# First batch's recurrence in half chunks of 64 tokens, in an mLSTM cell with Fourier mixing and an MLP

## The chip, the cores and the metric

One NeuronCore of a Trainium2 chip runs the whole program. The metric is the device time of one execution in microseconds (us); lower is better. Five engines take part, each with its own queue that is worked off in order: PE multiplies matrices into PSUM, DVE and ACT work on vectors (ACT also evaluates functions such as exp and tanh), POOL is a slower vector engine[...], and SP only issues DMAs. An instruction that waits for another engine holds everything behind it in its own queue.

## The reference

All inputs are float32. Batch B = 4, heads H = 8, tokens S = 768, head width D = 40, model width 320.

```python
def _attn_ref(q, k, v, i_gate, f_gate, o_gate):
    ...
    for t in range(S):
        kt, vt, qt = (k[:, :, t], v[:, :, t], q[:, :, t])
        m_new = np.maximum(f_gate[:, :, t] + m, i_gate[:, :, t])
        f_stab = np.exp(f_gate[:, :, t] + m - m_new)
        i_stab = np.exp(i_gate[:, :, t] - m_new)
        m = m_new
        C = f_stab[:, :, None, None] * C + i_stab[:, :, None, None] * np.einsum('bhd,bhe->bhde', vt, kt)
        n = f_stab[:, :, None] * n + i_stab[:, :, None] * kt
        h_tilde = np.einsum('bhde,bhe->bhd', C, qt)
        nq = np.einsum('bhd,bhd->bh', n, qt)[:, :, None]
        denom = np.maximum(np.abs(nq), 1.0)
        o = 1.0 / (1.0 + np.exp(-o_gate[:, :, t]))
        y[:, :, t] = o * h_tilde / denom

def _moe_ref(x, w_ch1, w_ch2):
    X = np.fft.fft(x, axis=1)
    X = np.fft.fft(X, axis=2)
    mixed = np.real(X).astype(np.float32)
    u = x + mixed
    mu = np.mean(u, axis=-1, keepdims=True)
    var = np.mean((u - mu) ** 2, axis=-1, keepdims=True)
    un = (u - mu) / np.sqrt(var + 1e-06)
    ch = np.maximum(un @ w_ch1, 0.0) @ w_ch2
    return (u + ch).astype(np.float32)
```

The output y of the cell, with its heads side by side, is the input x of the mixing stage.

## The kernel before

**Stages of a batch.** The recurrence over tokens is worked in six chunks of 128 tokens. Within a chunk, queries meet keys in a score matrix that is weighed with exponentials of gates and masked to the past; what came before the chunk arrives through a state of 40 x 41 numbers a head (the 41st column carries n). Then come the Fourier mixing (products with cosine and sine tables), the normalisation, and the two MLP products. The recurrence of batch b + 1 runs beside the MLP of batch b. Batch 0 has nothing to run beside: its gates, recurrence and mixing stand alone at the front.

**Two forms of the recurrence.** Batches 1 to 3 use `halves_*`: a chunk is two halves of 64 tokens; scores, state updates, from-state and from-chunk products are 64x64 tiles of PE, four of which can be under way at once (`TILES`, `product`, L518). Heads of one `hip` (0 to 3, 4 to 7) share a half of the partitions. Outputs have tokens on partitions, so `mlstm_finish` (L701, DVE: denominator, output gate, product) reads them from PSUM as they are. Chunks 0, 1 and 3 (`BACKWARDS`) are held in reverse order of tokens, which the mixing wants: `mlstm_finish` leaves them in `so` and `halves_rows` (L722) moves the rows into `x` by DMA. Batch 0 uses `mlstm_*` (L522 to L611): whole chunks of 128, two heads side by side, outputs with features on partitions; ACT copies them to `hT` (`mlstm_gather`, L577), PE turns them (`mlstm_turn`, L607), and only then DVE finishes them, straight into `x`.

**Gates** (`gates`, L142). For all 32 batch-heads at once, DVE sums the forget gates (`sums`), forms the running maxima M (`maxima`). PE spreads M over partitions for batch 0 (`spread_max`, L209: a mask product, then one product a head, from chunk 2 on in three bf16 parts that POOL makes in `parts`); ACT takes the exponential a head at a time, with a per-partition bias (`mlstm_exp`, L486, 8 x 128 columns a chunk). `weights` and `decay` on ACT make the factors of keys and queries; `columns` on PE turns the former, which lands in `colT`. The factors of queries and the maxima of later batches go out to DRAM (`G_d`, `M_d`) and come back spread over partitions (`Gb`, L472; `W`, L461). `halves_of_chunks` (L322) derives the factors for halves, which the later batches need.

**The order of work** is written by hand: `at(slot, phase, fn, ...)` puts a call into a plan; slots and phases are sorted, and each engine's queue gets its instructions in that order. Phases of a slot run from `EVAC` 0 over `FILL` 1, `MAIN` 2 to `FILL_PE` 3 and beyond. `gates` issues its first part at once, before slot 0. Batch 0's recurrence has slots 0 to 21, three a chunk (`plan_mlstm`, L742); its mixing starts at 22 (`plan_mix`, with folds of chunk pairs (2,3), (1,4), (0,5) at slots 16, 19, 22: `mix_fold`, L807, fold(2), fold(1), fold(0) below), its MLP at slot 31.

**SP's queue** issues all loads, in the order of the plan: a chunk's q and k (`mlstm_load`), `so` (output gate), `Gb`, the weight pieces, and the Fourier tables (`load_tables`, L437, slot 12, 1.8 MB). The MLP weights come as 64-bit words, in pieces of 640 KB: `load` (raw), `take` (two DVE instructions), `convert` (two on ACT), `join` (three on DVE). Five pieces are for w1 (numbers 0 to 4, number 2 being the tail `w1t_sb`); lists `when` (L1348) and `early` (L1358) say when.

Of the kernel before, what the change touches and what calls it, by code (L numbers as in the profile page):

```python
# [19 lines left out]
L = 128  # L20
# [33 lines left out]
def kernel(  # L54
# [28 lines left out]
    ps_early = ExitStack()  # L83
    ps_s, ps_h = (ps_early.enter_context(tc.tile_pool(name=n, bufs=2, space=PSUM)) for n in ("ps_s", "ps_h"))

    turn = iter("3210321032120312031230123012012301023130201320132013203120123021320321")
# [17 lines left out]
    h_first = const.tile([L, NP, 1], FP, name="h_first")  # L104
# [6 lines left out]
    C_bufs = [const.tile([L, NP, L], FP, name=f"C{n}") for n in range(3)]  # L111
    states = [t.rearrange("p n t -> p (n t)")[:, i * 2 * L:(i + 1) * 2 * L] for t in C_bufs for i in range(2)]
# [3 lines left out]
    Cd_bufs = [s_last[:, n * NP * D1:(n + 1) * NP * D1].rearrange("p (n m) -> p n m", m=D1) for n in range(2)]  # L116
    hT_bufs = [const.tile([L, NP, L], FP, name=f"h{n}") for n in range(2)]
# [18 lines left out]
    def idle_products(n, first=False):  # L136
        pw = bank("pi", [L, 2 * L]) if first else ps_s.tile([L, 2 * L], FP, name="pi", tag="ps")
        for i in range(n):
            nc.tensor.matmul(pw, rest[:, 0:L], rest, start=True, stop=True, skip_group_check=True)


    def gates(gp):  # L142
        f_sb = gp.tile([BH, NT, L], FP, name="f_sb")
        free = w2_sb.rearrange("p f m -> p (f m)")
        M, a = (free[0:n, (i + 1) * S:(i + 2) * S].rearrange("p (c t) -> p c t", t=L) for i, n in enumerate((L, BH)))
        nc.sync.dma_start(out=f_sb.rearrange("p c t -> p (c t)"), in_=f_gate.rearrange("b h s -> (b h) s"))
        nc.sync.dma_start(out=a.rearrange("p c t -> p (c t)"), in_=i_gate.rearrange("b h s -> (b h) s"))
        keep = gp.tile([BH, NT, L], FP, name="keep")
        shift = gp.tile([BH, NT, L], FP, name="shift")
        m_in = gp.tile([BH, NT, 1], FP, name="m_in")  # L150
        F = gp.tile([BH, NT, L], FP, name="F")
        g, wk = (x_bufs[1].rearrange("p c m -> p (c m)")[0:n, i * S:(i + 1) * S].rearrange("p (c t) -> p c t", t=L)
                 for i, n in enumerate((L, BH)))
        nM = gp.tile([BH, NT], FP, name="nM")
        M3 = gp.tile([3 * BH, NT, L], BF, name="M3")
        below = gp.tile([BH, NT, L], BF, name="below")
        sel = gp.tile([3 * BH, BH], BF, name="sel")
        ident_b, later_b = (gp.tile([L, L], BF, name=n) for n in ("ident_b", "later_b"))
# [7 lines left out]
        nc.gpsimd.memset(later_b, 0.0)  # L166
        nc.gpsimd.affine_select(out=later_b, in_=later_b, compare_op=OP.is_ge, fill=-M_INIT, base=0, pattern=[[1, L]],
                                channel_multiplier=-1)
        nc.scalar.copy(out=ident_b, in_=ident)
        for i in range(3):  # L170
            nc.scalar.copy(out=sel[i * BH:(i + 1) * BH], in_=ident[0:BH, 0:BH])
# [3 lines left out]
        nc.vector.memset(M[:, 0:2], 0.0)  # L175
        for t in C_bufs:
            nc.scalar.copy(out=t.rearrange("p (two n) t -> p two (n t)", two=2),
                           in_=rest.unsqueeze(1).to_broadcast([L, 2, 2 * L]))
# [7 lines left out]
        w1_pieces[1].load()  # L186
        for t in hT_bufs + Cd_bufs + [h_first]:
            nc.gpsimd.memset(t, 0.0)

        def flat(t, s):  # L190
            return t[0:BH, s].rearrange("p c t -> p (c t)")
# [5 lines left out]
        def maxima(s, initial):  # L197
            c0, c1 = s.start, s.stop
            nc.vector.tensor_tensor(out=a[:, s], in0=a[:, s], in1=F[:, s], op=OP.subtract)
            if c0 > 0:  # L200
                nc.vector.tensor_copy(out=shift[:, s, 0:1], in_=F[:, c0 - 1:c1 - 1, L - 1:L])
            nc.vector.tensor_tensor_scan(out=flat(M, s), data0=flat(shift, s), data1=flat(a, s), initial=initial,
                                         op0=OP.add, op1=OP.max)
            nc.vector.tensor_scalar(out=nM[:, s], in0=M[0:BH, s, L - 1], scalar1=-1.0, scalar2=None, op0=OP.mult)
            if c0 > 0:
                nc.vector.tensor_tensor(out=m_in[:, s], in0=M[0:BH, c0 - 1:c1 - 1, L - 1:L],
                                        in1=F[:, c0 - 1:c1 - 1, L - 1:L], op=OP.add)

        def spread_max(b, c, h0):  # L209

            k = chunks[b, c]
            if h0 == 0:
                k.W = wp.tile([L, H, L], FP, name="W", tag="W")
                k.M = []
            k.M.append(bank("pM", [L, NP, L]))
            nc.tensor.matmul(k.M[-1], ident_b, later_b.unsqueeze(1).to_broadcast([L, NP, L]), start=True, stop=False,
                             skip_group_check=True)
            for h in range(h0, h0 + NP):
                bh = b * H + h
                w, x = (ident[:, bh:bh + 1], M[:, c, :]) if c < 2 else (sel[:, bh:bh + 1], M3[:, c, :])  # L220
                nc.tensor.matmul(k.M[-1][:, h - h0, :], w.to_broadcast([w.shape[0], L]), x, start=False, stop=True,  # L221
                                 skip_group_check=True)

        def parts(s):

            m, rest_ = M[0:BH, s], shift[:, s]
            nc.gpsimd.tensor_copy(out=M3[0:BH, s], in_=m)
            nc.gpsimd.tensor_tensor(out=rest_, in0=m, in1=M3[0:BH, s], op=OP.subtract)
            nc.gpsimd.tensor_copy(out=below[:, s], in_=rest_)
            nc.gpsimd.tensor_copy(out=M3[BH:2 * BH, s], in_=rest_)  # L230
            nc.gpsimd.tensor_tensor(out=M3[2 * BH:, s], in0=rest_, in1=below[:, s], op=OP.subtract)

        def spread_decay(b, c):
            k = chunks[b, c]
            k.G = bank("pG", [L, NP, L])
            for h in range(H):
                r, bh = slice(h % 2 * 64, (h % 2 + 1) * 64), b * H + h
                nc.tensor.matmul(k.G[r, h // 2, :], ident[:, bh:bh + 1].to_broadcast([L, 64]), g[:, c, :],
                                 start=True, stop=True)

        def weights(s):
            for c in range(s.start, s.stop):
                nc.scalar.activation(out=wk[:, c], in_=a[:, c], func=AF.Exp, bias=nM[:, c:c + 1])

        def decay(s):
            for c in range(s.start, s.stop):
                nc.scalar.activation(out=g[0:BH, c], in_=M[0:BH, c], func=AF.Exp, scale=-1.0, bias=m_in[:, c])

        def columns(s, j):
            pt = ps_h.tile([L, NT, BH], FP, name="pt", tag="ph")  # L250
            for c in range(s.start, s.stop):
                nc.tensor.transpose(pt[:, c, :], (a, wk)[j][:, c, :], ident[0:BH, 0:BH])
            return pt

        first, others, last = slice(0, 1), slice(1, NT), slice(2, NT)
        sums(first)
        maxima(first, M_INIT)
        pt = columns(first, 0)
        nc.scalar.copy(out=colT[:, first, 0], in_=pt[:, first])
        weights(first)  # L260
        spread_max(0, 0, 0)
        pt = columns(first, 1)
        spread_max(0, 0, NP)
        mlstm_scores(0, 0)
        sums(others)
        mlstm_exp(0, 0, 0)
        nc.vector.tensor_copy(out=colT[:, first, 1], in_=pt[:, first])
        mlstm_exp(0, 0, NP)
        maxima(others, M[0:BH, 0, L - 1:L])
        pt = columns(others, 0)  # L270
        mlstm_load_o(0, 1)
        nc.vector.memset(g[:, 1:3], 0.0)
        nc.vector.tensor_copy(out=colT[:, others, 0], in_=pt[:, others])
        decay(slice(1, 2))
        weights(others)
        spread_max(0, 1, 0)
        spread_max(0, 1, NP)
        spread_decay(0, 1)
        pt = columns(others, 1)
        late = {"pt": pt}  # L280
# [5 lines left out]
        def columns_late():  # L286
            nc.vector.tensor_copy(out=colT[:, others, 1], in_=late["pt"][:, others])

        def decay_late():
            decay(last)  # L290
            nc.sync.dma_start(out=G_d[1:NT, 0:H].rearrange("c p t -> p c t"), in_=g[0:H, 1:NT])

        def decays():
            dec = gp.tile([BH, BH // 2, NT], FP, name="dec")
            nc.vector.tensor_tensor(out=dec[:, :, 1:],
                                    in0=g[0:BH, 1:, L - 1].unsqueeze(1).to_broadcast([BH, BH // 2, NT - 1]),
                                    in1=spread_sb[:, L:].unsqueeze(2).to_broadcast([BH, BH // 2, NT - 1]), op=OP.mult)
# [171 lines left out]
    def mlstm_queries(b, c):  # L469
        return slice(0, LH if b > 0 and c == 0 else L)  # L470
# [1021 lines left out]
```

## Time and profile before

| quantity | value |
|---|---|
| time, median of 3 runs | 392.07 us (391.45 to 392.17) |
| time of the profiled execution | 392.19 us |
| span of the profile | 390.4 us |
| busy over the span: PE / DVE / ACT / POOL | 379.6 / 278.0 / 172.1 / 134.9 us |
| first product of batch 0's MLP | 59.54 us |
| PE period of a chunk in batch 0 (c = 2 to 3) | 5.62 us |
| end of the last fold of batch 0 | 49.89 us |

The span runs from the first to the last instruction of the profiled execution, and the time includes what lies around it (1.8 us). A share of busy time is a mean over stages with different limits, so single windows of the timeline matter more here than the page. In the lines of the timeline the columns are start, duration (of a group: from its first start to its last end), engine, line, operation, output and inputs, number of instructions; in brackets the idle time before and what ended it. The ends of PE instructions are modelled, so groups that follow closely are measured start to start. A float32 matrix product appears as two instructions.

### The profile page before, as it was taken

The numbers are of one execution on the slowest core, as the hardware profiler recorded it, in microseconds if no ns is written. First come the engines' busy times: TensorE is split into PE (matmuls) and PEld (weight loads), VectorE is DVE, ScalarE is ACT, GpSimd is POOL, SyncE is SP. The second block draws the span as 40 slices with busy tenths as digits, with TensorE's granted clock in tenths as the row PEclk, the third lists the DMA queues.
The fourth block names the chain that finished last, engine by engine and source line by source line (L and its number), as shares of the span: only waits on it lengthen the run. The fifth ranks groups of instructions, "written<-read, shape, count | busy, mean of one in ns | idle before, by whom it ended". The sixth has DMA issues, their size and how long they took to land.

```text
span 390.4 us, 10585 instructions
## 1 busy us (share of the span) xinstructions
PE 379.6 (97%) x4174; PEld 277.3 (71%) x4174; DVE 278.0 (71%) x671; ACT 172.1 (44%) x481; POOL 134.9 (35%) x237
## 2 busy tenths in 40 slices
PE   8999899999999999999999999999999999999996
PEld 6777555656667777765569998755588996556996
DVE  7789988499599587476975699777655785346652
ACT  6887357477543233655462314554530133545000
POOL 5739504467954442173254134541500000020000
PEclk9999999999999999999999999999999999999999
DMA  7887499579394345437700626400000000000101
GB/s 224 287 235 204 159 254 255 179 214 271 109 231 116 122 116 150 149 102 184 182 2 28 174 80 192 135 20 2 0 2 34 6 30 34 2 0 0 35 34 35
DMA packets 25631, 44.78 MB, mean 115 GB/s; under 512 B 5727, under 2 KB 14766, under 8 KB 25454
## 3 DMA queue, kind: packets, MB, share of 16 engines
q1 hardware_dynamic: 25582, 44.11, 38.9%
q8 instruction: 33, 0.54, 0.6%
q14 instruction: 16, 0.13, 0.1%
HBM read 38.49 MB, written 4.12 MB: 109 GB/s over the span
## 4 chain that ended last, share of the span: by engine, by line
PE 78%; DVE 14%; issue 3%; ACT 3%; POOL 1%; DVEq 0%; ACTq 0%; POOLq 0%
PE po L1240 20%; PE pm L1121 15%; PE po L1184 8%; PE pm L1059 7%; PE ph L519 4%; PE pm L1126 4%; PE pu L938 4%; PE ps L519 3%; PE pm L1050 2%; PE put L981 2%; PE pz L907 1%; PE pz L895 1%; DVE h L1130 1%; DVE so L716 1%; PE pM L221 1%
## 5 line engine op out<-in xcount | busy, mean ns | idle before, releaser
L1190 DVE SCALAR_TENSOR_TENSOR x<-po,rstd,x 128x160 f32<-128x160 f32 (+1 forms) x69 | 27.1, 394 | 37.4 <-PE po L1240 32.5
L1130 DVE TENSOR_TENSOR h<-h,pm 128x384 f32<-128x384 f32 x60 | 30.5, 548 | 27.1 <-PE pm L1121 12.6
L652 POOL TENSOR_TENSOR C<-C,decB 128x164 f32<-128x164 f32 x30 | 15.9, 531 | 67.5 <-DVE C L667 56.1
L1121 PE MATMUL pm<-uT,w_sb 128*128 128x384 f32 x90 | 37.7, 506 | 1.3 <-DVE uT L1109 0.6
L491 ACT ACTIVATE W<-W,colT 128x64 f32<-128x64 f32 x144 | 37.5, 339 | 0.4 <-DMA W<-M_d 0.4
L1184 PE MATMUL po<-w_sb,h 128*128 128x320 f32 x120 | 34.3, 435 | 0.0
L515 POOL TENSOR_SCALAR_AFFINE_SELECT W<-W 64x512 f32<-64x512 f32 x36 | 27.3, 759 | 10.6 <-ACT W L491 9.1
L1005 POOL TENSOR_TENSOR t<-rstd 128x6 f32<-128x6 f32 x12 | 3.3, 273 | 79.9 <-DVE v L999 79.4
L1059 PE MATMUL pm<-uT,w_sb 128*128 128x384 f32 x80 | 29.2, 500 | 0.1
L1184 PEld LDWEIGHTS po<-w_sb,h 128*128 128x128 f32 x120 | 22.3, 190 | 9.5 <-issue 0.6
L1240 PE MATMUL po<-T,S 128*128 128x160 f32 x180 | 27.8, 301 | 0.3 <-DVE x L1190 0.3
L501 POOL TENSOR_TENSOR qg<-qk,Gb 128x512 f32<-128x512 f32 (+1 forms) x21 | 27.1, 1290 | 1.7 <-DMA qk<-in_qkT 1.6
L1240 PEld LDWEIGHTS po<-T,S 128*128 128x128 f32 x180 | 25.5, 190 | 1.7 <-DVE x L1190 0.5
L1121 PEld LDWEIGHTS pm<-uT,w_sb 128*128 128x128 f32 x90 | 15.5, 189 | 15.6 <-DVE h L1130 6.7
L1240 PE MATMUL po<-w_sb,h 128*128 128x160 f32 x180 | 26.3, 300 | 0.0
L1240 PEld LDWEIGHTS po<-w_sb,h 128*128 128x128 f32 x180 | 25.2, 190 | 1.4 <-DVE x L1190 0.3
L986 ACT COPY uT<-put 128x384 f32<-128x384 f32 x24 | 11.2, 477 | 30.1 <-PE put L981 30.1
L507 POOL TENSOR_TENSOR vw<-kvt,colT 128x328 f32<-128x328 f32 x23 | 19.7, 859 | 13.1 <-DMA qk<-in_qkT 10.1
L1177 ACT ACTIVATE h<-h 128x384 f32<-128x384 f32 x45 | 23.1, 520 | 2.0 <-DVE h L1130 2.0
L1126 PE MATMUL pm<-uT,w1t_sb 64*128 64x384 f32 x120 | 23.4, 508 | 0.0
L1059 PEld LDWEIGHTS pm<-uT,w_sb 128*128 128x128 f32 x80 | 14.1, 189 | 9.6 <-issue 1.9
L974 ACT ACTIVATE uc<-x 128x384 f32<-128x384 f32 x24 | 14.4, 613 | 12.6 <-DVE x L966 11.1
(241 smaller groups left out, 843.4 us busy)
## 6 DMA issues: line engine op xcount, KB each, us to landing
kvt<-in_kv SPq DMA_DIRECT2D x24, 336.0 KB
qk<-in_qkT SPq DMA_DIRECT2D x48, 160.0 KB
raw<-in_w SPq DMA_DIRECT2D x10, 640.0 KB
Gb<-G_d SPq DMA_DIRECT2D x36, 128.0 KB
W<-M_d SPq DMA_DIRECT2D x36, 128.0 KB
so<-in_o SPq DMA_DIRECT2D x24, 160.0 KB
out<-x SPq DMA_DIRECT2D x24, 160.0 KB
x<-so SPq DMA_DIRECT2D x9, 140.0 KB
```

The costliest lines, as they stand in the source:

```text
L491: nc.scalar.activation(out=k.W[:, h, :], in_=M, func=AF.Exp, scale=-1.0, bias=colT[:, c, 0, b * H + h:b * H + h + 1])
L501: nc.gpsimd.tensor_tensor(out=k.qg[:, :, t], in0=k.qk[:, 0, :, t], in1=k.Gb[:, :, t], op=OP.mult)
L515: nc.gpsimd.affine_select(out=W, in_=W, compare_op=OP.is_ge, fill=0.0, base=base, pattern=[[0, H], [step, LH]], channel_multiplier=-1)
L519: nc.tensor.matmul(out, w, x, start=start, stop=True, skip_group_check=True)
L1059: nc.tensor.matmul(k.pm[i], w1_sb[:, ch, f0:f0 + L], u[2 * ch], start=(ch == 0 and not ahead), stop=(ch == 1 and ahead), skip_group_check= ...
L1121: nc.tensor.matmul(bank, w, u, start=start, stop=True, skip_group_check=True)
L1126: nc.tensor.matmul(bank, block(w1t_sb, i)[rows], mlp_u(gr, 1)[rows], start=False, stop=True, skip_group_check=True)
L1130: nc.vector.tensor_tensor(out=h, in0=h, in1=bank, op=OP.add)
L1177: nc.scalar.activation(out=h, in_=h, func=AF.Relu, scale=-1.0)
L1184: nc.tensor.matmul(k.po[gr, i], hidden(gr, f)[:, i * L:(i + 1) * L], w2_sb[:, f, :], start=(f == 0), stop=(f == NFF - 1))
L1190: nc.vector.scalar_tensor_tensor(out=u, in0=po, scalar=k.rstd[:, c:c + 1], in1=u, op0=OP.mult, op1=OP.add)
L1240: nc.tensor.matmul(po, a[:, f], w[:, f], start=start and f == 0, stop=f == half - 1, skip_group_check=True)
```

## The change

Batch 0 gets the form of the other batches. `plan_mlstm`, its functions, `hT`, the padded states, `parts`, `halves_of_chunks`, `other_halves` and the separate PSUM pools go. The gates work in halves from the start, for all batches at once. The maxima of batch 0 are spread with the gates in the same sum, for half chunks, in float32, so that one exponential of 512 columns makes all weights of a chunk, mask included. The heads of batch 0 are copied from PSUM by ACT (`halves_heads`) before DVE finishes them, and chunks 0, 1 and 3 get their rows by DMA (`halves_rows`). Load order and the slots of the w1 pieces are new, with three raw buffers in place of two.

```diff
-    turn = iter("3210321032120312031230123012012301023130201320132013203120123021320321")
+    turn = iter("321031231203012030123012012301023130201320132013203120123021320321")
...
+        def in_order_of_queries(eng, c0, c1):
+            out, in_ = (t[:, c0:c1].rearrange("p c (i t) -> p (c i) t", i=2) for t in (m, M))
+            eng.tensor_copy(out=out, in_=backwards(in_, LH - 1, LH) if c0 in BACKWARDS else in_)
+
+        def weights(c):
+            for i in range(2):
+                nc.scalar.activation(out=halves(wk)[:, c, i], in_=halves(a)[:, c, i], func=AF.Exp, bias=nM[:, c, i:i + 1])
+
+        def decay(c):
+            for i in range(c == 0, 2):
+                nc.scalar.activation(out=gq[:, c, queries(c, i)], in_=halves(m)[:, c, i], func=AF.Exp, scale=-1.0,
+                                     bias=m_in[:, c, i:i + 1])
+
+        def spread_max(c):
...
+            k.M = bank("pM", [L, H, LH])
...
+            product(k.M, ident_b, later[:, int(c in BACKWARDS)].unsqueeze(1).to_broadcast([L, H, LH]), True)
+            product(k.M[:, 0:H:2], a[:, c], own[:, 0:H:2])
+            for j in range(2):
+                product(k.M[rows(j), 1:H:2], a[:, c, rows(1 - j)], own[:, 1:H:2])
+            for h in range(H):
+                for j in range(2):
+                    product(k.M[rows(j), h], ident[0:BH, h:h + 1].to_broadcast([BH, LH]), halves(m)[:, c, j ^ (h & 1)])
...
+        first, others = slice(0, 1), slice(1, NT)
         sums(first)
         maxima(first, M_INIT)
...
+        in_order_of_queries(nc.vector, 0, 1)
+        weights(0)
+        spread_max(0)
+        columns(0, 1, 1)
+        halves_scores(0, 0)
         sums(others)
...
+        mlstm_exp(0, 0)
+        columns_out(0, 1, 1)
+        decay(0)
+        mlstm_scale_v(0, 0)
+        maxima(others, M[:, 0, L - 1:L])
         mlstm_load_o(0, 1)
...
+        in_order_of_queries(nc.vector, 1, 2)
+        weights(1)
+        halves_to_state(0, 0)
+        spread_max(1)
+        columns(1, 2, 1)
+        decay(1)
+        spread_decay(0)
+        steps()
+        mlstm_exp(0, 1)
+        columns_out(1, 2, 1)
+        halves_weigh(0, 0)
+        halves_add(0, 0, 0)
+        steps_out()
+        halves_decay(0, 0, 1)
+        mlstm_scale_v(0, 1)
+        for c0, c1, _ in RUNS[1:]:
+            in_order_of_queries(nc.gpsimd, c0, c1)
+        mlstm_scale_q(0, 0)
+        halves_add(0, 0, 1)
+        spread_decay(1)
...
+        for s, phase, f, args in (
+                (1, FILL, weights, (2,)), (1, FILL + 0.1, decay, (2,)), (1, FILL + 0.2, decay, (3,)),
+                (1, FILL + 0.3, weights, (3,)), (1, FILL + 0.4, decay_out, (1, 4, 0)), (3, FILL_PE + 4, spread_decay, (2,)),
+                (3, FILL_PE + 5, columns, (2, 4, 1)), (4, FILL + 0.3, columns_out, (2, 4, 1)), (4, FILL + 0.4, weights, (4,)),
+                (4, FILL + 0.5, decay, (4,)), (5, FILL + 0.4, weights, (5,)), (5, FILL + 0.5, decay, (5,)),
+                (5, FILL + 0.6, decay_out, (4, 6, 0)), (5, FILL + 0.65, decay_out, (0, 1, H, slice(0, LH))),
+                (6, FILL_PE + 5, columns, (4, 6, 1)), (7, FILL + 0.3, columns_out, (4, 6, 1)), (6, FILL + 0.9, maxima_out, ()),
+                (9, FILL_PE + 5, columns, (0, 6, 0)), (10, FILL + 0.3, columns_out, (0, 6, 0)),
...
         for c in range(2, NT):
...
+            at(3 * c - 3, FILL_PE + 3.5, spread_max, c)
...
-    def mlstm_exp(b, c, h0):
+    def mlstm_exp(b, c, h0=None):
 
         k = chunks[b, c]
+        if b == 0:
+            weights_of(k)
+            nc.scalar.activation(out=k.W, in_=k.M, func=AF.Exp, scale=-1.0)
+            return
...
+    def halves_heads(b, c):
+
+        k = chunks[b, c]
+        h = tp.tile([L, 2, NP, D1], FP, name="heads", tag="heads")
+        nc.scalar.copy(out=h, in_=k.ph)
+        k.ph = h
...
-        k.x = k.so if b > 0 and c in BACKWARDS else xs[b][:, c, 0:DM]
+        k.x = k.so if c in BACKWARDS else xs[b][:, c, 0:DM]
...
+    def plan_first():
         for c in range(NT):
...
+            s = 3 * c
+            if c > 1:
+                at(s - 2, FILL, mlstm_exp, 0, c)
+                at(s - 1, FILL, mlstm_scale_v, 0, c)
             if c > 0:
...
+                at(s, FILL + 0.1, mlstm_scale_q, 0, c)
+                at(s, FILL_PE + 2.05, halves_scores, 0, c)
+                at(s, FILL_PE + 2.5, halves_to_state, 0, c)
+                at(s + 1, FILL - 0.3, halves_weigh, 0, c)
+                for i in range(2):
+                    at(s + i, FILL + 0.05, halves_decay, 0, c, i)
+                    at(s + 1 + i, FILL - 0.2, halves_add, 0, c, i)
             end = c == NT - 1
...
+            t = s + 2 if end else s + 3
+            at(t, FILL_PE, halves_from_state, 0, c)
+            at(t, FILL_PE, halves_from_chunk, 0, c, 0)
+            at(t, FILL_PE + 0.5, halves_between, 0, c)
+            at(t, FILL_PE + 0.6, mlstm_tanh, 0, c)
+            at(*((19, FILL_PE) if end else (t, FILL_PE + 3)), halves_from_chunk, 0, c, 1)
+            at(20 if end else t + 1, FILL - 0.5, halves_heads, 0, c)
+            at(*((21, FILL + 0.05) if end else (17 if c == 4 else t + 1, FILL + 0.3)), mlstm_finish, 0, c)
+            if c < 4:
+                at(s + 5, FILL - 0.6, halves_rows, 0, c)
...
-    when = [((2, 0.7), (4, 0.5), (6, 0.6)), ((6, 0.7), (7, 0.5), (8, 0.6)), ((11, 0.7), (13, 0.5), (22, 0.6))]
-    when += [((22, 0.7), (23, 0.7), (31, 0.5)), ((31, 0.7), (32, 0.7), (33, 0.6))]
+    when = [((5, 0.7), (6, 0.7), (8, 0.6)), ((17, 0.7), (18, 0.7), (22, 0.6)), ((22, 0.7), (23, 0.7), (31, 0.5))]
+    when += [((31, 0.7), (32, 0.3), (33, 0.6)), ((33, 0.65), (34, 0.1), (35, -0.1))]
...
-    early = [(3, mlstm_load, 3), (3, mlstm_load_o, 2), (4, mlstm_load, 4), (5, mlstm_load_decay, 3),
-             (5, mlstm_load_decay, 4), (6, None, 2), (7, mlstm_load_o, 3), (7, mlstm_load, 5),
-             (11, mlstm_load_decay, 5), (11, None, 3), (11, mlstm_load_o, 4), (12, load_tables, None),
-             (14, mlstm_load_o, 5), (23, None, 4)]
+    early = [(3, mlstm_load, 3), (3, mlstm_load_o, 2), (3, mlstm_load_decay, 3), (5, mlstm_load, 4), (6, mlstm_load_o, 3),
+             (7, mlstm_load_decay, 4), (7, None, 1), (8, mlstm_load, 5), (9, mlstm_load_decay, 5), (9, mlstm_load_o, 4),
+             (10, None, 2), (12, load_tables, None), (12, mlstm_load_o, 5), (13, None, 3), (23, None, 4)]
...
```

In `early`, `None, n` is the load of w1 piece n. `maxima_out` and `decay_out` write `M_d` and `G_d` on SP's queue, as before but earlier. The order of the arrays that the host prepares follows the new layout.

## The prediction

> **What bounds the kernel now.** The page's slices come first: PE is busy 8 to 9 tenths everywhere, which says little, so the next view is busy time by stage.
>
> ```profile
> 30.00:40.00 10.00, 9.74 (x142) 8.34 (x142) 9.38 (x24) 7.27 (x24) 8.96 (x14) 1.00 0.75 224
> 40.00:50.00 10.00, 8.21 (x55) 5.08 (x54) 9.24 (x25) 3.32 (x8) 5.20 (x11) 1.00 0.40 145
> 60.00:70.00 10.00, 10.00 (x97) 5.51 (x95) 7.60 (x11) 7.38 (x22) 5.20 (x6) 1.00 0.99 267
> ```
>
> Columns: window, PE, PE's weight loads, DVE, ACT, POOL, clock, DMA share, GB/s. From 60 us PE is full. Batch 0's first MLP product starts at 59.54 us, and what follows is a stream of products that the change leaves alone. So the change is worth what it moves that start. The timeline of DVE shows what holds it:
>
> ```profile
> 29.88 0.16 DVE L712 TENSOR_SCALAR den<-px 128x8 f32<-128x8 f32 x1
> ...
> 41.30 0.74 DVE L815 TENSOR_TENSOR eo<-x 128x320 f32<-128x320 f32 x1
> ...
> 46.40 0.15 DVE L712 TENSOR_SCALAR den<-px 128x8 f32<-128x8 f32 x1
> ...
> 48.21 0.49 DVE L815 TENSOR_TENSOR eo<-x 128x320 f32<-128x320 f32 x1
> ...
> 49.57 0.32 DVE L822 TENSOR_TENSOR fe<-eo 128x159 f32<-128x159 f32 x1
> 49.81 0.82 DVE L420 SCALAR_TENSOR_TENSOR e<-raw,e 128x640 uint32<-128x640 uint32 x1
> ```
>
> Nearly without a pause from 29.88 to 49.89 us DVE finishes six chunks and folds three pairs. The last fold ends at 49.89; DFT, turns and first product follow 9.65 us later. That stretch stays as it is: what the change takes from it (the `colT` and `decB` copies at 57.29) lies after the third turn that the first product needs. Measure of the change: **where does the last fold end?**
>
> Two more timelines, of PE and of the DMA queue on SP:
>
> ```profile
> 10.10 1.16 PE L221 MATMUL pM<-w_sb,ident 128*128 128x128 f32 x8
> 11.10 0.38 PE L216 MATMUL pM<-later_b,ident_b 128*128 128x512 bf16 x1
> 11.31 1.05 PE L221 MATMUL pM<-w_sb,ident 128*128 128x128 f32 x8
> 12.30 1.09 PE L238 MATMUL pG<-x,ident 128*64 128x128 f32 x16
> ...
> 63.16 0.69 PE L519 MATMUL ps<-qk 40*64 40x64 f32 x32
> 63.68 0.63 PE L519 MATMUL ps<-vw,kvt 64*64 64x41 f32 x32
> ```
> ```profile
> 32.17 3.62 SPq L320 DMA_DIRECT2D M_d<-w_sb  x4
> 35.83 0.58 SPq L438 DMA_DIRECT2D ds_sb<-in_dft_s  x1
> 36.46 0.43 SPq L439 DMA_DIRECT2D dd_sb<-in_dft_d  x1
> 37.00 0.36 SPq L484 DMA_DIRECT2D so<-in_o  x1
> 45.44 2.14 SPq L343 DMA_DIRECT2D G_d<-x  x4
> ```
>
> Start to start, a float32 instruction of 128 columns takes 124 ns (8 in 0.99), two 64-column tiles side by side halve that (16 in 1.02), and four 64x64 tiles take 16.3 ns each (32 in 0.52). After the table issue at 35.83, one-microsecond windows show the DMA engines busy up to 42.7.
>
> **What the Trainium skill says.** "TensorEngine Tiling (Array Packing)", Key Properties: different tiles load weights and multiply in parallel; the trace agrees (124, 64 and 16 ns above). "DMA: Bandwidth & Descriptors", Anatomy of one DMA: DMA engines don't wait on semaphores, the issuing sequencer does; the trace agrees: SP issues nothing from 12.7 to 16.10 while it waits to write `G_d`, with the load of chunk 4 behind it. The same page, Queues, rings and completion order: on each DMA engine descriptors are taken in ring order. No wait of this trace shows that clearly; I rest the forecast on it.
>
> **The change part by part.**
>
> *PE.* Before, a chunk costs turn 0.5, from-state 0.98, scores 1.09, from-chunk 0.9, to-state 0.7, maxima 0.9 (bf16): 5.1, in a period of 5.62. After: four groups of 32 instructions at 16.3 = 2.1. The maxima become dear: mask 0.21, two of 256 columns at 0.24 = 0.48, four of 256 columns in two tiles 0.72, 32 of 64 columns, two tiles at a time, at 65/2 ns = 1.04; 2.45 in all. Period 4.6 plus small transposes, about 5.0. The maxima's 32-row tiles are not in the trace: bounds 2.0 (four at a time) and 3.4 (none beside another); I take 2.45.
>
> *ACT.* Exponentials 2.17 a chunk become one of 512 columns, about 0.6 (the 512-column copy L597 takes 0.59); state copies 0.61 go; a head copy of about 0.45 and "between" 0.14 come. But the gates' weights and decays, now 32x64, come in slots 1, 4 and 5, two of each a chunk at about 0.25, in front of "between", for which PE waits.
>
> *DVE.* Weigh 1.28 becomes 0.68 (L672); two state sums of 0.32 come (L667); a finish stays 1.7. One w1 piece (take 0.9 to 1.7, join 2.4 to 3.5) moves from the recurrence to the MLP, slots 31 to 35, where DVE has room (7.6 of 10). Its joins come just before PE wants the columns (slots 35, 36): bounds 0 and +1.5, I take 0.
>
> *POOL.* Parts (4.1), the other batches' halves (about 6) and the old decays (1.0 a chunk) go; two decays of 0.53 and 1.2 of reversing come. Not the bound, save below.
>
> *Walk.* The first maxima start at 4.2 and run at half speed up to 6.6 as the old ones did (1.84 for eight against 1.0): end 7.9. Exponential 8.5, `colT` 9.1, vw 10.1, to-state 10.6, second maxima 13.1, pG(0) 13.7, pd 14.1, `decB` 14.45. On POOL, decay, vw and reversing stand behind `decB`: 16.3 for chunk 2. ACT's decays of chunks 2 and 3 end at 17.3, weights(3) at 17.8; PE, which waits for "between" before the rest of from-chunk, resumes at 18.05 (1.2 lost). Maxima(2) 20.6, pG 21.6, columns 21.75. ACT then does three copies (0.6), eight gate operations (2.1) and the w1 convert (1.5): decay(5) is done at 24.5, "between" of chunk 1 at 26.1. PE loses another 2.2. From there, at about 5.0 a chunk, scores(5) end near 39.9, the state sum of chunk 5 at 41.2: DVE is ready for the first fold then, as against 41.30 before. What PE saves a chunk is lost in the two waits.
>
> *After it, on DVE:* fold(2) 1.2, finish(4) 1.7, take 0.9, fold(1) 1.2, finish(5) 1.7, fold(0) 1.7 = 8.4. PE's side (POOL 1.1, DFT 1.4, the late half of from-chunk 0.3, head copy 0.6) is within the first 5.0 of it. So without further waits: 49.6, or -0.3.
>
> *SP.* Here is a new wait: the backwards chunks 0, 1 and 3 now get their rows by DMA, and fold(2) needs chunk 3's. All loads stand in one order. `G_d` of chunks 1 to 3 (slot 1) holds the queue up to 17.35, so the engines go empty, while before they were full up to 15. `G_d` of chunks 4, 5 holds it up to 24.5. From there: `G_d` 0.6, qk and kv 1.1, so 0.35, `M_d` 3.6, Gb 1.25, raw 0.45, two row moves at 0.56 (L728), qk and kv 1.1, Gb 1.25, so 0.35, raw 0.45, one row 0.56 = 12.2; tables at 36.7. Before, tables and the `so` behind them were through 6.9 after their issue: 43.6. Behind them a raw of 640 KB (at the 0.4 MB/us of that stretch) 1.6, then the rows: 0.4 and about 0.4 to land: **46.0**. Bounds: 42.8 if tables are issued as soon as finish(2) frees rows(2), about 34; 48.5 if earlier loads still fill the rings, whose sum from 32 us on is near 8 us of transfers before the tables. I take 46.0. DVE stands from 41.2 to 46.0; behind the first fold stand finish(4), the take, fold(1), finish(5) and fold(0). Last fold 46.0 + 8.4 = 54.4, against 49.89: +4.5. A second hold agrees in direction: `so` of chunk 5 lands near 43.8 and its tanh stands before the convert and the head copy on ACT.
>
> Sum: the profiled execution took 392.19 (span 390.4); 392.19 + 4.5 = 396.7. The median is 392.07, 0.12 less, which I neglect.
>
> **Rivals.**
> 1. *Faster, four tiles win.* If row moves are not kept behind tables and w1, and the maxima take 2.0, scores(5) come 1.8 earlier (four maxima at 0.45): last fold 47.8, 392.19 - 2.1 = 390.1. For it: three finishes (5.1) leave DVE's full stretch, ACT has 1.5 less a chunk. It decides if chunk 3's rows land before about 40. Against it: SP's sum above.
> 2. *No change.* Rows land before 41.2, maxima as priced: 392.19 - 0.3 = 391.9. For it: DMA engines are empty at 43 to 45 now, so there is some room; against it the same sum.
> 3. *PE bound.* Maxima at 3.4 each: five times 0.95 = 4.75 on PE, 41.2 becomes 46, and SP's two holds move by 1.9, so rows land near 48: last fold 56.3, 392.19 + 6.4 = 398.6. For it: no view shows a 32-row tile; against it: two column tiles do overlap at L238.
> 4. *Little of the change works*, exponentials still in parts or tiles one after another: the diff has one activation a chunk and L519 shows the tiles overlapping; no chance of its own.
>
> **How the numbers follow.** Forecast (rows queued behind the tables) 0.50, own range 394.5 to 399.5; PE bound 0.15; no change 0.13; faster 0.22. A measurement of this kernel tells about 0.2% (0.8 us) from no change; its three runs lie within 0.7. Of the no-change case a quarter falls on faster; the rest and a little of its neighbours is within: faster 0.25, same 0.10, slower 0.65. Range 389.5 to 399.5: below it lies the end of the faster case, above it the end of the PE-bound one.
>
> **What would show it.** Right: on DVE an idle gap of 3 to 6 us before the first L815 with a DMA of `x` as releaser, SP at the tables near 37, chunk 3's row moves after them, and a last fold near 54. The two PE waits for "between" (1.2 and 2.2) at 17 and 24 us. Maxima of 2.45 from start to start. Wrong: the first fold starts right after the state sum; or maxima of 2 us; or the MLP starts before 59.

## The result, and the profile after

| | before | after |
|---|---|---|
| time, median | 392.03 us (391.45 to 392.17) | 415.53 us (414.51 to 417.18, 4 runs) |
| ratio, 95% interval | | 1.0606 (1.0568 to 1.0645) |
| span of the profiled execution | 390.4 us | 412.8 us |
| first product of batch 0's MLP | 59.54 us | 77.23 us |
| from there to the end of the span | 330.9 us | 335.6 us |

The change makes the kernel slower by 6%. Of the 22.4 us that the span grows, 17.7 lie ahead of the first MLP product and 4.7 behind it. The direction was forecast, the size was not: 396.7 was expected, in a range that ended at 399.5. In experiments 2 and 7 below one run of four was a slow one (405.02 and 433.96 us), which their figures and ratios leave out.

Three rows of the page of after, the first two for its 40 slices of 10.3 us:

```profile
PEclk9985558999989999999999999999999999999999
DMA  7257981957958525334670064530000000000010
...
q8 instruction: 37, 0.61, 0.6%
```

The clock row is all nines before the change. Now it shows TensorE (PE's array) at half its clock in slices 4 to 6. By stage, with the columns used above (window, its length, PE, weight loads, DVE, ACT, POOL, clock, DMA share, GB/s):

```profile
30.00:40.00 10.00, 8.76 (x186) 6.95 (x186) 6.48 (x12) 3.55 (x11) 4.24 (x7) 0.50 0.61 166
40.00:50.00 10.00, 10.00 (x178) 7.34 (x176) 4.25 (x13) 2.65 (x8) 4.42 (x8) 0.50 1.03 305
50.00:60.00 10.00, 8.54 (x199) 7.25 (x198) 4.51 (x11) 2.13 (x6) 4.15 (x8) 0.50 0.95 301
60.00:70.00 10.00, 9.39 (x44) 4.21 (x44) 9.57 (x21) 2.97 (x6) 3.79 (x6) 0.76 0.05 9
```

Before, DVE had 9.38 of ten microseconds in the first of these windows; now it has 6.48, and PE has become the bound at half speed. PE's timeline shows what that costs, with the maxima of chunk 2 and of chunk 4; "32*64" is a weight tile of 32 rows and 64 columns:

```profile
23.29 0.61 PE L224 MATMUL pM<-later,ident_b 128*128 128x512 bf16 x1
23.83 1.27 PE L224 MATMUL pM<-own,w_sb 32*128 32x256 f32 x6
24.94 1.10 PE L224 MATMUL pM<-w_sb,ident 32*64 32x64 f32 x32
25.87 1.04 PE L240 MATMUL pG<-x,ident 32*64 32x128 f32 x16
...
31.24 0.66 PE L476 MATMUL ph<-kvt,W 64*64 64x41 f32 x16 [1.34 <-ACT warm L573]
...
39.94 0.61 PE L224 MATMUL pM<-later,ident_b 128*128 128x512 bf16 x1
40.48 2.26 PE L224 MATMUL pM<-own,w_sb 32*128 32x256 f32 x6
42.54 1.92 PE L224 MATMUL pM<-w_sb,ident 32*64 32x64 f32 x32
44.38 0.84 PE L248 MATMUL pt<-ident,w_sb 32*128 32x32 f32 x6
...
77.23 2.85 PE L939 MATMUL pm<-uT,w_sb 128*128 128x384 f32 x8
```

Start to start, the maxima take 2.58 us in the one short stretch that is mostly at full clock (23.29 to 25.87) and 4.44 us otherwise (39.94 to 44.38). From maxima to maxima a chunk takes 8.1 us (31.84 to 39.94), against a forecast of about 5.0. DVE's side, the folds:

```profile
57.78 0.49 DVE L695 TENSOR_TENSOR eo<-x 128x320 f32<-128x320 f32 x1 [1.12 <-DMA x<-so]
...
67.85 0.33 DVE L702 TENSOR_TENSOR fe<-eo 128x159 f32<-128x159 f32 x1
68.09 0.82 DVE L375 SCALAR_TENSOR_TENSOR e<-raw,e 128x640 uint32<-128x640 uint32 x1
```

The first fold starts at 57.78 instead of 41.30. The wait for chunk 3's rows, on which the forecast rested, is there with the releaser that was named, but is 1.12 us long. The last fold ends at 68.18, and the first MLP product follows 9.05 us later. SP's queue says why the wait is short:

```profile
44.40 0.58 SPq L393 DMA_DIRECT2D ds_sb<-in_dft_s  x1
...
46.71 0.33 SPq L351 DMA_DIRECT2D raw<-in_w  x1
51.36 2.06 SPq L602 DMA_DIRECT2D x<-so  x3
```

Tables and raw weights do stand ahead of the rows, but the slow recurrence finishes chunk 3 so late that SP waits 4.3 us after the raw issue before it can issue them.

The last 4.7 us are in batch 1:

```profile
115.29 0.51 PE L476 MATMUL ps<-vw,kvt 64*40 64x41 f32 x32
118.32 0.44 PE L476 MATMUL ph<-kvt,W 64*64 64x41 f32 x16 [2.52 <-issue]
118.69 4.54 PE L939 MATMUL pm<-uT,w_sb 128*128 128x384 f32 x8
```

PE stands for 2.52 us, "issue" meaning that the profile shows no releaser (experiment 11 tells what it is), and the eight MLP products behind it take 4.54 us instead of the 2.85 of those at 77.23, since the clock has fallen after the pause (0.86 in 120 to 130 us). 2.52 + 1.69 = 4.21 of the 4.7.

### The profile page after: what moved, and what is told of

The parts are those of the page before. It is cut to its first block, busy times and chain, and to the rows that moved or that the text cites. A ratio compares the mean times of both kernels' runs of the same rounds, so it can differ in the third digit from the quotient of the medians.

```text
span 412.8 us, 11639 instructions
## 1 busy us (share of the span) xinstructions
PE 398.4 (97%) x4724; PEld 288.2 (70%) x4724; DVE 275.7 (67%) x673; ACT 161.9 (39%) x449; POOL 128.0 (31%) x224
## 4 chain that ended last, share of the span: by engine, by line
PE 73%; DVE 13%; DMA 6%; issue 3%; ACT 3%; POOL 1%; SPq 1%; DVEq 0%; POOLq 0%
PE po L1120 18%; PE pm L1001 14%; PE po L1064 8%; PE ph L476 5%; PE pM L224 5%; PE pm L939 4%; PE ps L476 4%; PE pm L1006 4%; DMA qk<-in_qkT 3%; PE pu L818 2%; DMA kvt<-in_kv 2%; PE pz L775 1%; DVE h L1010 1%; PE pm L930 1%; PE put L861 1%
## 5 line engine op out<-in xcount | busy, mean ns | idle before, releaser
L519 POOL TENSOR_TENSOR C<-C,decB 128x164 f32<-128x164 f32 x40 | 21.5, 538 | 89.2 <-DVE C L534 59.3
L1001 PE MATMUL pm<-uT,w_sb 128*128 128x384 f32 x90 | 37.7, 506 | 1.3 <-DVE uT L989 0.6
L939 PE MATMUL pm<-uT,w_sb 128*128 128x384 f32 x80 | 30.9, 524 | 0.1
L539 DVE TENSOR_TENSOR W<-ps,W 128x512 f32<-128x512 f32 x24 | 16.4, 685 | 18.8 <-PE ps L476 18.7
L476 PE MATMUL ph<-kvt,W 64*64 64x41 f32 x768 | 24.2, 248 | 4.7 <-issue 2.5
L1001 PEld LDWEIGHTS pm<-uT,w_sb 128*128 128x128 f32 x90 | 15.5, 189 | 15.6 <-DVE h L1010 6.7
L476 PEld LDWEIGHTS ph<-kvt,W 64*64 64x64 f32 x768 | 19.6, 155 | 7.9 <-issue 2.6
```

The source lines that it names most:

```text
L476: nc.tensor.matmul(out, w, x, start=start, stop=True, skip_group_check=True)
L939: nc.tensor.matmul(k.pm[i], w1_sb[:, ch, f0:f0 + L], u[2 * ch], start=(ch == 0 and not ahead), stop=(ch == 1 and ahead), skip_group_check= ...
L1001: nc.tensor.matmul(bank, w, u, start=start, stop=True, skip_group_check=True)
```

## The experiments

Lines in diffs are those of the kernel that was edited. "Theory A" is: the clock falls because the maxima and decays now use 32 of the array's 128 rows. "Theory B" is: it falls because PE idles in waits.

**1. The changed kernel, maxima and decays on 128 rows, rows 32 to 127 zero.**

```diff
-            product(k.M[:, 0:H:2], a[:, c], own[:, 0:H:2])
+            product(k.M[:, 0:H:2], a_all[:, c], own[:, 0:H:2])
...
-                    product(k.M[rows(j), h], ident[0:BH, h:h + 1].to_broadcast([BH, LH]), halves(m)[:, c, j ^ (h & 1)])
+                    product(k.M[rows(j), h], ident[:, h:h + 1].to_broadcast([L, LH]), halves(m_all)[:, c, j ^ (h & 1)])
```

> The kernel after the change, with the operands of the spread maxima and decays on all 128 partitions, rows 32 to 127 zero: same instructions, same columns, same waits. Theory A (the TensorE clock follows how many rows of the array work): it stays full from about 7 us on, maxima take 2.5 us in every chunk in place of 4.4, the MLP starts at 60 to 65 us and the time is 394 to 400. Theory B (the clock falls because PE idles in waits for ACT and DVE): the waits are all still there, the clock is half from about 28 us on as before, and the time is 412 or more.

Measured: 413.37 us, ratio 1.0513 (1.0459 to 1.0567). The total hardly moves: theory A's 394 to 400 failed, and the total alone would fit theory B. The profile tells them apart. Windows, DVE's timeline and SP's queue:

```profile
24.00:27.00 3.00, 1.51 (x19) 0.98 (x19) 0.92 (x5) 2.24 (x6) 1.46 (x5) 0.80 0.65 153
27.00:30.00 3.00, 3.00 (x45) 2.26 (x46) 2.93 (x6) 0.20 (x1) 1.56 (x2) 0.63 0.77 241
30.00:40.00 10.00, 9.60 (x378) 8.19 (x380) 7.51 (x18) 4.35 (x15) 5.39 (x8) 1.00 0.72 187
40.00:50.00 10.00, 3.93 (x137) 3.21 (x129) 0.96 (x3) 1.35 (x5) 2.39 (x3) 0.64 1.02 365
```
```profile
54.41 0.49 DVE L703 TENSOR_TENSOR eo<-x 128x320 f32<-128x320 f32 x1 [9.83 <-DMA x<-so]
```
```profile
43.09 2.31 SPq L610 DMA_DIRECT2D x<-so  x3
```

PE does 378 products in the window where it did 186. DVE is ready for the first fold at 44.58 instead of 56.66, and then everything stands: the rows are issued at 43.09, with tables and raw weights ahead of them and the DMA engines full, and DVE waits 9.83 us. This is the forecast's mechanism, twice as large as forecast. With idle time the clock falls again: after a wait of PE of 2.10 us (before 25.49; 0.80 and 0.63 above), and for longer around the hold. So 128 rows don't keep the clock up through waits. The clock's loss hid the DMA's, and repairing one alone uncovers the other.

**2. The kernel before, maxima of chunks 0 and 1 and the decays on 32 rows.** The other direction: no work and no wait is added, the zero rows are left out.

```diff
-                w, x = (ident[:, bh:bh + 1], M[:, c, :]) if c < 2 else (sel[:, bh:bh + 1], M3[:, c, :])
+                w, x = (ident[0:BH, bh:bh + 1], M[0:BH, c, :]) if c < 2 else (sel[:, bh:bh + 1], M3[:, c, :])
```

> The kernel before the change, with the spread maxima of chunks 0 and 1 and the spread decays of chunks 1 and 2 on 32 rows in place of 128 (of which 96 were zero). Theory A: PE stays at half speed beyond 6.6 us, the maxima of chunk 1 take about 2 us for eight instructions in place of 1.05, the front is 1 to 4 us longer: 393 to 396. Theory B: nothing changes, 392.

Measured: 396.98, 397.20 and 399.52 us, ratio 1.0150 (1.0114 to 1.0186), more than the 393 to 396 expected. Two windows of its trace:

```profile
9.00:12.00 3.00, 3.00 (x14) 2.21 (x13) 1.94 (x6) 1.92 (x7) 2.79 (x5) 0.50 1.04 343
15.00:18.00 3.00, 3.00 (x29) 2.60 (x27) 0.95 (x3) 1.75 (x7) 0.50 (x1) 0.50 0.78 267
```

PE has work in every microsecond, and still its clock is halved, up to about 22 us. The first MLP product comes at 64.52 instead of 59.54. So the clock can fall without idle time, with only the rows changed.

**3. The changed kernel with eight 128-row products of zeros among each chunk's maxima.**

> The kernel after the change, with one product of zeros, 128 rows by 128 columns, 92 columns long, after each head of the spread maxima (eight a chunk, 1.4 us at full clock, 2.9 at half). Theory A: a third of the maxima now uses all rows, so the clock may come back; then the time is 400 to 406. Theory B: the fillers fill no idle time, the clock stays half and the time is 425 or more.

Measured: 458.57 us (one run). PE's timeline:

```profile
39.10 0.42 PE L224 MATMUL pM<-w_sb,ident 32*64 32x64 f32 x4
39.46 0.73 PE L233 MATMUL ps<-rest 128*128 128x92 f32 x2
40.12 0.48 PE L224 MATMUL pM<-w_sb,ident 32*64 32x64 f32 x4
```

The fillers take 0.66 of each 1.02 us here and the maxima stay slow. Zero products on 128 rows between the 32-row ones do not bring the clock back; products with data were not tried.

**4. Shift of the instruction stream, first try**: 64 one-column products at the start of the changed kernel.

> The changed kernel with 64 one-column zero products (64 weight loads and 64 matmuls, 128 instructions for TensorE) put at the very start, where TensorE has no data yet. Nothing else moves. The question is the 2.52 us for which TensorE stands at 115.80 before the second turn of a head product, released by nothing that the profile shows. In the trace of the changed kernel 3521 TensorE instructions stand in the record before that pause, and in that of the first experiment (pause 112.79 to 116.65) 3521 as well; the queue that fetches TensorE's instructions (256 in one packet) has a packet at 115.50 to 116.81 in the one and at 114.22 to 115.37 in the other, and TensorE goes on 1.5 and 1.3 us after its end. Theory F (the pause is a late instruction fetch, behind loads of batch 1): with the packets' borders 128 instructions earlier in the program, the pause leaves this place; the time falls by the pause and by the half-speed stretch after it, some 3 to 5 us, to about 411, unless another border now falls on a burst of small products, in which case a pause of 1 to 4 us stands at another place but again before a multiple of 256 instructions. Theory G (a hidden wait, for the state's sum on DVE that ends at 118.31 or for GpSimd's chain): the pause stays before the same product, 2 to 4 us long, time 414 to 417.

Measured: 442.65 us, ratio 1.1305 (1.1270 to 1.1340). A miss: a float32 product of one column runs as two instructions with two weight loads, so the 64 took 27.3 us, and they were 256 instructions, a whole packet. The pause (1.97 us) stayed before the same product. Theory F allows that, so nothing was told apart. But the 27.3 us of zero products left TensorE at half speed too: the maxima behind them (31.14 to 35.56) take 4.42 us.

**5 and 6. Tables and w1's second piece early, its fourth piece behind chunk 3's rows**; on the changed kernel, and on the kernel with 128 rows.

```diff
         mlstm_load_o(0, 1)
+        load_tables()
+        w1_pieces[1].load()
...
-             (10, None, 2), (12, load_tables, None), (12, mlstm_load_o, 5), (13, None, 3), (23, None, 4)]
+             (10, None, 2), (12, mlstm_load_o, 5), (14, None, 3), (23, None, 4)]
```

> The changed kernel (32-row maxima) with the two DFT tables and the second piece of w1 issued right after the second chunk's output gates (SP at about 9 us, where the DMA is idle afterwards) and the fourth piece of w1 behind chunk 3's rows instead of ahead of them, so that these rows don't stand behind 1.8 MB of tables and 0.64 MB of raw weights. Theory A (the array's clock carries the loss, the DMA hold is hidden behind it): the first batch stays at half speed, the wait for the rows before the fold (1.12 us in the changed kernel) goes, the first MLP product comes 0 to 2 us earlier, time 412 to 416. Theory D (the DMA hold carries a large part): time at or under 408.

> The first experiment's kernel (maxima and decays' operands on 128 rows, the added rows zero) with the same moves of DMAs as in the run before. In the first experiment DVE stood 9.83 us at the fold for chunk 3's rows, issued at 43.1 and landed at 54.4, and the clock fell after it. Theory A with the forecast's mechanism as second limit: rows land within 4 us of their issue, the hold shrinks from 9.8 to under 3 us, the first MLP product comes at 62 to 67 instead of 74, and the time is 398 to 406. If the hold were not the tables' doing (other traffic): hold over 6 us and time over 408.

Measured: 412.53 us, ratio 1.0528 (1.0485 to 1.0570), and 401.14 us, ratio 1.0235 (1.0213 to 1.0256). With the two kernels above this makes a square, medians in us and the first MLP product in brackets:

| | tables as in the change | tables early |
|---|---|---|
| maxima, decays on 32 rows | 415.53 (77.23) | 412.53 (78.11) |
| on 128 rows | 413.37 (74.32) | 401.14 (66.99) |

Neither repair moves the first MLP product by over 3 us alone; together they move it by 10.2. (In the fifth kernel chunk 2's maxima and decays take 6.15 us, 23.28 to 29.43, where the changed kernel's short fast stretch has 3.55; without that loss early tables would gain it about 1.7 us, by my estimate.) Of the sixth kernel, PE's and DVE's timelines:

```profile
27.28 0.39 PE L232 MATMUL pM<-later,ident_b 128*128 128x512 bf16 x1
27.51 1.18 PE L232 MATMUL pM<-own,w_sb 128*128 128x256 f32 x6
28.52 1.10 PE L232 MATMUL pM<-w_sb,ident 128*64 128x64 f32 x32
29.55 0.31 PE L256 MATMUL pt<-ident,x 32*128 32x32 f32 x2
```
```profile
47.18 0.49 DVE L705 TENSOR_TENSOR eo<-x 128x320 f32<-128x320 f32 x1 [2.20 <-DMA x<-so]
```

The maxima take 2.27 us, and the hold falls from 9.83 to 2.20. The rows still land only 5.6 us after their issue (41.59 to 47.18), against under 4 expected.

**7. The sixth kernel with the shift of experiment 4.**

> The run before with the 64 one-column zero products at the start. Theory F: 3 to 8 us under the run before (pause of 3.87 us and the half-speed stretch of about 2 us after it gone), 393 to 402. Theory G: no difference over 1 us. Theory A also allows a small gain at the start, since the products keep TensorE at work before the first data: clock at full speed before 7 us.

Measured: 425.69, 427.42 and 427.91 us, ratio 1.0901 (1.0868 to 1.0934). The same 27.3 us of zero products; by itself it tells nothing of theory F.

**8. ScalarE's gate work and w1's conversion out of the way of "between", two pieces of w1 behind the rows**, on the sixth kernel.

```diff
-                (3, FILL_PE + 5, columns, (2, 4, 1)), (4, FILL + 0.3, columns_out, (2, 4, 1)), (4, FILL + 0.4, weights, (4,)),
-                (4, FILL + 0.5, decay, (4,)), (5, FILL + 0.4, weights, (5,)), (5, FILL + 0.5, decay, (5,)),
+                (3, FILL_PE + 5, columns, (2, 4, 1)), (4, FILL + 0.3, columns_out, (2, 4, 1)), (4, FILL + 0.1, weights, (4,)),
+                (4, FILL + 0.15, decay, (4,)), (4, FILL + 0.2, weights, (5,)), (4, FILL + 0.25, decay, (5,)),
...
```

> The kernel with the tables early and 128 rows (401.14 us), and two more moves: ScalarE's four gate activations of chunks 4 and 5 into the 2.63 us for which it waited at 20.2 us, and the conversion of the first piece of w1 behind the one-element read between two turns, so that TensorE no longer waits 2.10 us at 24.81 for that read; and the loads of the third and fourth piece of w1 behind chunk 3's rows, so that 0.64 MB less stands ahead of them (DVE waited 2.20 us for the rows at 47.18). Theory A with waits as second limit: the 2.10 us goes, the hold for the rows falls under 1 us, the clock doesn't fall at 40 or stays down more briefly, time 395 to 399. If waits of this kind don't matter: 400 to 402.

Measured: 401.90 us (398.81 to 403.55), ratio 1.0246 (1.0194 to 1.0298). The 2.10 us wait is gone, but just ahead of its place PE now waits 1.43 us for GpSimd's scaling of the values, which stands behind ScalarE's four operations. The hold for the rows is 1.19 us. The first MLP product came at 65.23, 1.76 us earlier; then PE paused for 2.68 us in batch 1 (104.20 to 106.88), where the sixth kernel's pause was 1.59. The expectation of 395 to 399 failed.

**9 and 11. A shift of about half a packet**, with 64 small bf16 products, on the eighth kernel and on the changed kernel.

```diff
-        idle_products(3, True)
+        idle_products(1, True)
+        rest_b = rest.bitcast(BF)
+        for i in range(64):
+            nc.tensor.matmul(scores[0:32, 0, 0:1], rest_b[:, 0:32], rest_b[:, 0:1], start=True, stop=True, skip_group_check=True)
```

> The run before, with two of the three wide zero products at the start replaced by 64 products of bf16, 32 columns of weights and one of data: one weight load and one matmul each, 128 instructions for 8 (the shift tried first was of 256 instructions, one whole packet, since every float32 product runs as two passes of a load and a matmul, and those 64 products took 27.3 us for their weights). In the run with the tables early TensorE was held 1.91 us at 20.23 in the middle of a row of like products, and 1.59 us at 100.08, each ending 1.4 to 1.7 us after a packet of instructions. Theory F: those pauses move to other products; by how much the time changes depends on where the borders fall, 2 us less to 3 us more. Theory G: the pauses stay before the same products.

> The changed kernel with the same 64 small bf16 products at the start for two of the three wide ones (120 instructions more, with the two products' eight fewer). Theory F (the pause of 2.52 us at 115.80 is a late instruction fetch): no pause before instruction 3521 of the old count; if one stands, it stands about 120 instructions earlier or 136 later than there, time 409 to 417. Theory G: the pause of 2 to 4 us stays before the same head product.

Measured: 401.35 us, ratio 1.0239 (1.0219 to 1.0258), and 414.89 us, ratio 1.0598 (1.0569 to 1.0627). In both the pause in batch 1 is gone, and in both a new one stands at one and the same later place. The ninth kernel has four more in batch 0 (1.38, 1.29, 1.03 and 0.51 us; the eighth had two there, 0.92 and 0.46). Of the eleventh kernel (the changed one, shifted), PE's timeline:

```profile
117.42 0.51 PE L479 MATMUL ps<-vw,kvt 64*40 64x41 f32 x32
117.79 0.44 PE L479 MATMUL ph<-kvt,W 64*64 64x41 f32 x16
...
271.64 0.35 PE L479 MATMUL ph<-kvt,W 64*64 64x41 f32 x9
273.37 0.32 PE L479 MATMUL ph<-kvt,W 64*64 64x41 f32 x7 [1.38 <-issue]
```

The product that waited 2.52 us now waits for nothing, though DVE's and GpSimd's instructions beside it are the same. The new pause splits sixteen like products after the ninth, where no engine's result is needed. By the trace's DMA packets, one of instructions for PE ran from 270.99 to 271.97, and PE went on 1.4 us after its end. Theory G falls. Theory F had expected a new pause close to the old place, which failed, but a count confirms it. Count PE's recorded instructions (loads, products, semaphores) in order of start: all 27 pauses that end in "issue", in eleven of the fourteen traces, stand before instruction 193 above a multiple of 256. PE is at 256k + 193 when it goes on, 1.2 to 1.7 us after the end of its k-th packet. In the changed kernel that is 3521 (k = 13, after a packet that ended at 116.81), here 7873 (k = 30), in the ninth 705, 961, 1473, 1729 and 7873:

```profile
35.12 0.81 PE L235 MATMUL pM<-w_sb,ident 128*64 128x64 f32 x21 [1.03 <-issue]
```

None stands in batch 0 of the kernels that are at half speed there (the changed one, 4, 5, 10, 11): the slow clock seems to have hidden these waits as well. The total hardly gains: a pause moved rather than vanished. And in this profile the first MLP product came at 79.75, 2.5 us later than in the changed kernel, and the missing fast stretch accounts for it: chunk 2's maxima and decays took 6.15 us (23.50 to 29.65) instead of 3.55 (23.29 to 26.84).

**10. The sixth kernel with 64 rows instead of 128.**

> The kernel with the tables early (401.14 us), with the maxima's and decays' operands on 64 rows instead of 128 (rows 32 to 63 zero). Theory A says that the clock follows the rows in use: with half of them it should be held at half speed for part of the first batch, between the two kernels: 403 to 410. If any use of more than one group of 32 rows is enough: 400 to 402. If only all rows count: 411 to 414.

Measured: 413.40 us, ratio 1.0547 (1.0532 to 1.0563), as with 32 rows. PE's timeline:

```profile
12.02 2.27 PE L232 MATMUL pM<-own,w_sb 64*128 64x256 f32 x6
14.08 1.92 PE L232 MATMUL pM<-w_sb,ident 64*64 64x64 f32 x32
```

Half speed, as in the changed kernel. Half of the rows is not enough, and theory A's "between the two" was wrong.

**12. The sixth kernel with only the maxima on 128 rows.**

> The kernel with the tables early (401.14 us), with only the maxima's operands on 128 rows, and the decays' 32-row products (about 1.1 us of a period of 4.4 to 5 us) as in the changed kernel. It tells which of the 32-row products hold the clock down. If what counts is a mean of the rows in use over some time, the maxima (2.3 us of a period) carry most of it: 401 to 405, with half speed in the first 7 us or after single chunks only. If any stretch of 1 us on 32 rows sets the clock back: 408 to 414, at half speed throughout.

Measured: 401.45 us, ratio 1.0271 (1.0233 to 1.0308), the first MLP product at 67.50. The maxima alone decide the time. In this kernel's profile the clock is lower in batch 0 (0.83 in 10 to 20 us and 0.79 in 20 to 30, where the sixth kernel has 1.00), which costs next to nothing here.

No version came under the kernel before: the best is 401.14 us.

## Why the prediction was wrong

- **The step that failed** is the first sentence of the walk: "The first maxima start at 4.2 and run at half speed up to 6.6 as the old ones did", and all that follows at full speed. The old maxima of the first two chunks were products on 128 rows, the new ones on 32, and with them TensorE stayed at half speed until 23 us and again from 27 to about 65. The forecast priced the 32-row tile (2.45 us, bounds 2.0 and 3.4), but not what it does to the clock of all products around it: 2.27 to 2.58 us was right at full clock, 4.44 was measured. The four-tile groups of 32, taken at 0.5 us, took 0.9 (36.62 to 37.50). So DVE was ready for the first fold at 56.66 instead of 41.2.
- **The clock.** The Trainium skill, "TensorE: Matmul & The Clock Gate", Part 1, says that the clock is halved by default and that a busy stretch of about 3.4 us releases it. The start of the kernel before is like that: PE works from 1.25 us and is at full speed from 6.6, 5.3 us later. The trace of after differs: 10.00 of 10 us busy (40 to 50 us) and a clock of 0.50. The measurement decides: being busy was not enough here, and with the maxima on 128 rows the clock came back.
- **The DMA hold** was right in kind and wrong in size and place. Forecast: rows land at 46.0 and DVE stands 4.8 us. In the changed kernel it is 1.12, hidden behind PE; with the clock repaired 9.83: the rows landed 11 us after their issue, behind tables that were issued at 39.97 instead of 36.7, into full DMA engines. That the loads moved in experiment 6 caused it is shown by the fall to 2.20; which of them did, tables or w1 pieces, is not.
- **The waits for "between"**: the first (1.2 us) does not show. The second (2.2 us, chunk 1) is 1.34 us in the changed kernel and 2.10 us in the sixth.
- **The period** of about 5.0 us is 4.42 us in the sixth kernel from chunk 3's maxima (27.28) to chunk 4's (31.70), without waits, and 6.8 to the next, with waits in it.
- **From the first fold to the end of the last** 8.4 us were forecast; it took 10.4 (57.78 to 68.18), and 10.5 in the sixth kernel, so 2 us were missing there. **The stretch behind the last fold** was taken as unchanged at 9.65 us, and is 9.05. The ledger of the changed kernel is thus 56.66 + 1.12 + 10.40 + 9.05 = 77.23, against 41.2 + 4.8 + 8.4 + 9.65 = 64.05.
- **Batch 1 and later** were taken as "a stream of products that the change leaves alone". They lost 4.7 us. The products are the same, but PE waits there for a packet of instructions; that was in no step and no rival.
- **The rivals.** "PE bound" named the engine that became the bound, through maxima of 3.4 us each, and put the end at 398.6; the cause was another one, and it reached all products of the stretch.

What stays open: what exactly sets the clock back. Maxima on 32 and 64 rows did, on 128 they did not; zeros in the added rows served, but the zero products of experiments 3 and 4 did not. Whether the number of rows counts or the form of tile that goes with it was not separated. The 2.10 us wait before 25.49 lowered the clock in the first kernel, and one of the same length before 26.91 did not in the sixth (1.00 in 20 to 30 us). And of the 7.5 us by which the sixth kernel's first MLP product is late (66.99 against 59.54), the profile names a pause of 1.91, a wait of 2.10, a hold of 2.20 and half clock in the folds (0.70 in 50 to 60 us), which were not all taken away singly.

## What to carry to other kernels

Price a small tile by what it does to the clock of its neighbours too: if short products on few rows replace products on all 128, look at the duration of an unchanged product beside them, and try the same operands padded with zero rows. When two limits stand one behind the other, removing either alone shows almost nothing; test them in a square. Many tiny products also need many instructions, and those come by DMA: if an engine pauses in the middle of like products with no releaser, count its instructions and see whether the pauses lie whole blocks apart.

## What the runs showed that was not expected

- **Instructions are a DMA load.** PE's 9,448 instructions of the changed kernel (4,724 products and as many weight loads) come by the queue q8 on the page: 0.61 MB in 37 packets, about 256 instructions each, as the pauses of experiment 11 confirm. The Trainium skill, "Runtime: NRT & Kernel Launch", Instruction fetch mechanics, gives the same block size and calls the cost of crossing a border mostly hidden. Here it wasn't, mostly where small products ran at full clock: in the first experiment PE ran dry at 112.79, the packet began only at 114.22 and ended at 115.37, and PE went on at 116.65.
- **The clock row can be wrong.** For the tenth kernel the record gives a clock of 1.0 throughout, while its maxima take 2.27 and 1.92 us, the durations of half speed; in after, the same holds for the first 20 us. The durations of a known product are the surer sign.
- **A product of one column can be dear**: 0.43 us each for the 64 float32 products of experiment 4, with 128 columns of weights, whereas the bf16 products of experiments 9 and 11 with 32 columns of weights took 29 ns (64 in 1.87 us). Type and columns changed together, so their shares are not known.
